# Moving early zero stores and weight loads between steps of one DMA queue: gated linear attention followed by a top-2 expert router on one core

## The chip, the core and the metric

The kernel runs on one core of one Trainium2 chip. The core has a matrix engine (TensorE, "PE" in the profile, with "PEld" for its weight loads), three engines for elementwise work (VectorE "DVE", ScalarE "ACT", GpSimd "POOL") and SyncE ("SP"), which here does nothing but send DMA transfers. POOL also sends DMA transfers, the indirect ones that gather or scatter rows by an index list. All transfers of the core run on the same 16 DMA engines. The metric is the device time of one execution in microseconds (us); lower is better.

## The reference, cut to what matters

There are two blocks. The first is a recurrent attention over 4 batches, 8 heads, 768 positions and a head width of 48:

```python
f = 1.0 / (1.0 + np.exp(-f_logit))
for t in range(S):
    state = f[:, :, t, :, None] * state + np.einsum('bhd,bhe->bhde', k[:, :, t], v[:, :, t])
    y[:, :, t] = np.einsum('bhd,bhde->bhe', q[:, :, t], state)
```

Its output is reshaped to x with 3072 tokens of 384 features. The second block is a router with 8 experts, each of which is a 384 x 1024 x 384 network with a ReLU. For every token the two experts with the largest noisy logits are chosen and weighted by a softmax over the two:

```python
noisy_logits = x @ w_gate + np.log1p(np.exp(x @ w_noise)) * noise
# top2, top2_w: the two largest and their softmax weights
for e in range(E):
    for k in range(2):
        mask = top2[:, k] == e
        out[mask] += top2_w[mask, k, None] * (np.maximum(x[mask] @ w1[e], 0.0) @ w2[e])
```

All data are float32.

## The kernel before, in words

**Attention.** The sequence is cut into 6 chunks of 128 positions; chunk and batch together give NS = 24 blocks, n = 4 * chunk + batch. The loop at line 1285 runs steps i = -3 to 25. In each step seven stages run, each on a block of its own: `forget(i+3)`, `scaled(i+1)`, `scores(i)`, `summed(i+2)`, `output(i-1)`, `decays(i+2)`, `features(i-2)` (a stage whose block does not exist is skipped). So `output(n)` is in step n+1 and `features(n)` in step n+2. `features(n)` (line 629) makes the 128 rows of x that belong to block n in the tile `xs`; they are stored to the DRAM buffer `x_rows` by SP, in the step that follows (the list `xw`, line 639).

**The order of the queue.** `in_order` (line 1205) keeps each engine's instructions in the order in which the program was written, so SP's transfers go out in exactly this order. In each step SP sends the loads of f, q, k and v for blocks three to four ahead (`load`, line 525, 192 KB each, in runs of 192 bytes), the store of the last step's x rows (line 639, 192 KB), in some steps a small load of noise (line 505), and then what the lines 1310 to 1318 add. Those lines are what the change touches. They send two kinds of transfers for which nothing in the attention waits:

- `zeros(count)` (line 1250) stores zeros into `count` blocks of 128 rows of the output (line 1254, 192 KB each). The results of the experts are later added into those rows, so the zeros have to be there first. The first twelve such stores cover the rows of the first half of each batch (chunks 0 to 2), the other twelve the second half. In the kernel before, the first twelve are sent in steps 6 to 13 (one each, after `output(5)` to `output(12)`) and in steps 22 and 23 (two each). The other twelve are sent after the loop, in the expert stage (line 1363).
- `part_of_weights(k, which, part)` (line 838) loads a quarter, 384 KB, of the first or second weight matrix of expert k. Expert 0's w1 goes in steps 14 to 17, one part each; its w2 in steps 18 and 19, two parts each (one after `output`, one after `features`); expert 1's w1 in steps 22 to 25.

**Routing.** After each chunk, `route(c)` (line 642) picks the two experts of each token and hands out eight indirect stores (`put`, line 708, sent by POOL at line 710), which write the tokens into the experts' lists in DRAM. When the lists of chunks 0 to 2 are written, the first expert pairs can begin although the attention still runs: `first_loads` (line 1259) sends, on SP, the look-up of the first 256 entries of expert 0's list (`fetch`, line 815, tile `slots`), then on POOL the gather of the token rows (`gather`, line 826, tile `xg`, in two halves of 128 tokens), and lets PE transpose the rows (`turned`, line 862, tile `xgp`). The look-up for expert 0 comes in step 20, right behind that step's store of x rows and its load of v. Its gather comes in step 21, its first transposes in step 22 after `output(21)`; steps 22 to 25 then hold both the last attention blocks and the first matmuls of expert 0 (line 914).

**Experts.** After the loop the list of items runs: four experts on their first 256 tokens, and then all experts on the rest, with products arranged in seven instead of eight multiplications (lines 939 and 1021). Each item ends with indirect stores on POOL that add the rows into the output (line 1030); those of the first four experts wait for the first twelve zero stores.

Of the kernel before, what the change touches and what calls it, by code (L numbers as in the profile page):

```python
# [331 lines left out]
def kernel(  # L332
# [192 lines left out]
    def load(nm, n):  # L525
        c, b = n // B, n % B
        if n < NCH * B:
            nc.sync.dma_start(out=pads[nm][n % RING[nm]][:, :, 0:D],
                              in_={"f": f_logit, "q": q, "k": k, "v": v}[nm][b, :, c * C:(c + 1) * C, :].rearrange("h t d -> t h d"))

    def clamp(n, engine=nc.gpsimd):
        if n < NCH * B:
            raw = pads["f"][n % RING["f"]][:, :, 0:D]
            engine.tensor_scalar(raw, raw, XMIN, None, ALU.max)
# [303 lines left out]
    def part_of_weights(k, which, part):  # L838
        if which == 1:
            few = slice(part * FF // 4, (part + 1) * FF // 4)  # L840
            nc.sync.dma_start(out=w1[k][:, :, few], in_=moe_w1[k].rearrange("(k p) f -> p k f", p=128)[:, :, few])
        else:
            few = slice(part * FO // 4, (part + 1) * FO // 4)
            nc.sync.dma_start(out=w2[k][:, few], in_=moe_w2[k].rearrange("(f p) d -> p f d", p=128)[:, few])
# [389 lines left out]
    NS = NCH * B  # L1234
# [15 lines left out]
    def zeros(count):  # L1250
        for _ in range(count):

            m = (*(m for m in range(NS) if m % NCH < HALF), *(m for m in range(NS) if m % NCH >= HALF))[len(zeroed)]
            zeroed.append(nc.sync.dma_start(out=out[m * 128:(m + 1) * 128, :], in_=zero))
            if m % NCH >= HALF:
                tc.declare_no_dep(zeroed[-1].ins, group="first half", reason="rows differ")
                tc.add_to_no_dep_group("second half", zeroed[-1].ins)
# [27 lines left out]
    for i in range(-3, NS + 2):  # L1285
        for stage, lag in ((forget, -3), (scaled, -1), (scores, 0), (summed, -2), (output, 1), (decays, -2), (features, 2)):
            n = i - lag
            if not 0 <= n < NS:
                continue
            stage(n)  # L1290
            if stage is forget:
                load("f", n + 4)
                clamp(n + 2, nc.gpsimd if n else nc.vector)
            elif stage is scaled:
                for nm in "qk":
                    load(nm, n + 2) if n < 4 else load(nm, n + 3)
                    if n == 3:
                        load(nm, n + 3)
                if n < 2:
                    load_router(n)  # L1300
                while xw:
                    xw.pop(0)()
            elif stage is scores:
                for m in (n + 1,) if n < 4 else (2 * n - 3, 2 * n - 2) if n < 6 else (n + 3,):
                    load("v", m)
                if n in (2, 6, 7, 8, 9, 10):
                    load_router(2 + (2, 6, 7, 8, 9, 10).index(n))
                elif n == 5:
                    nc.sync.dma_start(out=lists.rearrange("(p r) w -> p r w", p=128), in_=empty)
            elif stage is output:  # L1310
                if 5 <= n < 13:
                    zeros(1)
                elif n in (21, 22):
                    zeros(2)
            for when, first_n, last_n, whose, layer, part in ((output, 13, 16, 0, 1, 0), (output, 17, 18, 0, 2, 0),
                                                              (features, 16, 17, 0, 2, 2), (features, 20, 23, 1, 1, 0)):
                if stage is when and first_n <= n <= last_n:
                    part_of_weights(whose, layer, part + n - first_n)
            next(router, None)
            slot += 1  # L1320
            if puts and slot % (2 if n_routed == HALF else 3) == 0:
                puts.pop(0)()
            next(first_pairs, None)

            if done["turned"] and (n_first < 5 or i >= NS - 3 and stage is not forget) and (n_first < 11 or i >= NS - 1):
                next(pieces)
                n_first += 1
        if i < 0:
            warm_up(4)
        if i >= NS - 1:  # L1330
            while xw:
                xw.pop(0)()
        n = i - 2
        if n >= 0 and n % B == B - 1:
            c = n // B
            router = chain(router, route(c))
            n_routed = c + 1
            if c == HALF - 1:
                router = chain(router, enough())
                first_pairs = first_loads()  # L1340
            if c == NCH - 1:
                router = chain(router, plan(), beyond())
# [18 lines left out]
    for item, piece in pieces:  # L1361
# [6 lines left out]
        n = item - NE - 2  # L1368
# [52 lines left out]
```

## Time and profile before

| | |
|---|---|
| time, median of 3 runs | 662.32 us (660.88 to 662.96) |
| the profiled execution's own time | 667.17 us |
| its span, first to last instruction | 665.4 us |
| mean granted TensorE clock | 0.985 |
| ACT, POOL busy | 254.6 us (38%), 266.9 us (40%) |
| DMA, mean rate over the span | 145 GB/s |
| packets under 512 bytes | 115600 of 153897 |
| zero stores (`out_dram<-zero`) | 24, 192.0 KB each |
| weight parts (`w<-in_moe_w_dram`) | 16, 384.0 KB each |
| attention with DMA, 10 to 140 us | 132 to 230 GB/s in stretches of 10 us |

The durations come from one profiled execution, which took 4.85 us longer than the median of the timed runs. A line of a timeline gives the start in us from the span's start, the duration, the engine ("SPq" is SyncE sending a DMA), the line of the kernel, the operation, and the tiles as out<-in. For SPq the duration is the time for which SyncE was held by sending, not the time of the transfer. The chain of waits runs from the last instruction back to what released it. In the table by stretch, the last numbers are the granted clock of TensorE, the mean busy share of the DMA engines (the sum of packet times, so it can pass 1), and what they moved.

Step i is found in the trace by its scores (line 580): step 14's start at 92.76 us, step 19's at 125.09, step 20's at 130.69, step 22's at 141.04.

### The profile page before, as it was taken

The page shows a single profiled execution, that of the slowest core. Times are in us where ns is not written, and L with a number is a line of the kernel's source. Part 1 is how long each engine was busy: PE and PEld are TensorE (multiplying, and loading weights), DVE is VectorE, ACT ScalarE, POOL GpSimd, SP SyncE. Part 2 cuts the span into 40 slices and gives each one's busy share as a digit, 9 for nine tenths or more (in the row PEclk, how much of TensorE's full clock was granted, in tenths as well). Part 3 has the DMA queues.
Part 4 walks back from the last instruction along what each step waited for, and adds up shares of the span by engine and source line. Part 5 has one row for each costly group of instructions (what it writes and reads, how often), then busy time and mean ns, then how long its engine had stood idle before and what let it go on. Part 6 is the DMA issues. An engine that isn't in the chain of part 4 may idle for free.

```text
span 665.4 us, 12898 instructions
## 1 busy us (share of the span) xinstructions
PE 637.2 (96%) x4883; PEld 550.1 (83%) x4883; DVE 441.8 (66%) x993; ACT 254.6 (38%) x603; POOL 266.9 (40%) x300
## 2 busy tenths in 40 slices
PE   7999999967999999999999999999999999999991
PEld 7999988856999998999858965995698579889891
DVE  7777867853457666787666676757576667766751
ACT  5876766731221233333233333333322332232320
POOL 7633888715077623261521450325034214413021
PEclk9999999997999999999999999999999999999997
DMA  9999887893599423465725760836184337602112
GB/s 183 190 220 230 187 168 150 186 250 101 168 330 224 106 47 69 118 184 201 222 86 170 170 167 25 292 46 189 26 288 97 91 116 211 180 3 25 22 25 29
DMA packets 153897, 96.31 MB, mean 145 GB/s; under 512 B 115600, under 2 KB 146320, under 8 KB 153824
## 3 DMA queue, kind: packets, MB, share of 16 engines
q1 hardware_dynamic: 141648, 76.12, 41.6%
q0 software_dynamic: 12176, 19.25, 15.3%
q8 instruction: 41, 0.67, 0.4%
q14 instruction: 32, 0.26, 0.1%
HBM read 75.97 MB, written 19.62 MB: 144 GB/s over the span
## 4 chain that ended last, share of the span: by engine, by line
PE 93%; DMA 3%; issue 1%; DVE 1%; POOL 0%; SPq 0%; ACT 0%; POOLq 0%; DVEq 0%
PE y L1021 32%; PE P L939 8%; PE hp L914 6%; PE W L939 5%; PE Z L939 5%; PE V L939 5%; PE X L939 5%; PE xp L633 4%; PE sc L580 4%; PE y L598 4%; PE xgp L862 2%; PE y L609 2%; PE kp L540 2%; PE fp L540 1%; PE qp L540 1%; PE ds L604 1%
## 5 line engine op out<-in xcount | busy, mean ns | idle before, releaser
L1030 POOL DMA_INDIRECT out_dram<-ys,slots x48 | 81.8, 1705 | 154.1 <-ACT ys L1088 131.8
L1021 PE MATMUL y<-qk_all,f_all 128*128 128x192 f32 x576 | 105.2, 327 | 0.0
L1021 PEld LDWEIGHTS y<-qk_all,f_all 128*128 128x128 f32 x576 | 93.3, 190 | 0.3 <-DVE f_all L1003 0.3
L826 POOL DMA_INDIRECT xg<-x_rows,slots x48 | 53.5, 1114 | 50.5 <-DMA slots<-lists 34.1
L1021 PE MATMUL y<-w,hs_b 128*128 128x192 f32 x320 | 59.1, 328 | 0.0
L710 POOL DMA_INDIRECT lists<-entry,sloti x48 | 52.0, 1083 | 10.3 <-issue 9.9
L1021 PEld LDWEIGHTS y<-w,hs_b 128*128 128x128 f32 x320 | 52.9, 190 | 0.9
L1162 POOL DMA_INDIRECT out_dram<-ys_q,slots_q x5 | 8.6, 1718 | 104.0 <-DVE ys_q L1160 104.0
L914 PE MATMUL hp<-xt_a,w 128*128 128x256 f32 x192 | 43.7, 383 | 0.0
L975 ACT ACTIVATE hs_b<-hs_b 128x256 f32<-128x256 f32 (+1 forms) x32 | 15.1, 472 | 71.7 <-DVE hs_b L955 68.4
L914 PEld LDWEIGHTS hp<-xt_a,w 128*128 128x128 f32 x192 | 35.8, 190 | 4.9 <-issue 0.3
L939 PE MATMUL X<-xt_a,w 128*128 128x256 f32 (+1 forms) x128 | 39.7, 432 | 0.0
L939 PE MATMUL Z<-xt_b,v_all 128*128 128x256 f32 (+1 forms) x128 | 39.7, 432 | 0.0
L583 DVE TENSOR_TENSOR A<-sc,causal 128x1024 f32<-128x1024 f32 x24 | 29.3, 1222 | 13.4 <-PE sc L580 7.3
L1088 ACT ACTIVATE ys<-ys,slots 128x384 f32<-128x384 f32 x24 | 14.8, 617 | 59.7 <-DVE ys L1087 49.5
L1080 DVE TENSOR_TENSOR ys<-P,y 128x192 f32<-128x192 f32 x24 | 8.5, 354 | 42.2 <-PE y L1021 29.0
L955 DVE TENSOR_TENSOR hs_b<-hs_a,X 128x256 f32<-128x256 f32 (+1 forms) x32 | 15.6, 487 | 29.9 <-PE X L939 29.8
L1021 PE MATMUL y<-w,f_all 128*128 128x192 f32 x192 | 35.1, 326 | 0.0
L862 PE MATMUL xgp<-ident,xg 128*128 128x128 f32 x144 | 24.3, 279 | 9.9 <-DMA xg<-x_rows,slots 9.9
L939 PEld LDWEIGHTS X<-xt_a,w 128*128 128x128 f32 x128 | 24.3, 190 | 10.1
L939 PEld LDWEIGHTS Z<-xt_b,v_all 128*128 128x128 f32 x128 | 24.3, 190 | 10.1
L955 DVE TENSOR_TENSOR hs_a<-hs_a,P 128x256 f32<-128x256 f32 (+1 forms) x64 | 31.1, 486 | 1.4
(199 smaller groups left out, 1445.1 us busy)
## 6 DMA issues: line engine op xcount, KB each, us to landing
w<-in_moe_w_dram SPq DMA_DIRECT2D x16, 1536.0 KB
w_q<-in_moe_w_dram SPq DMA_DIRECT2D x10, 1536.0 KB
w<-in_moe_w_dram SPq DMA_DIRECT2D x16, 384.0 KB
f_all<-in_f_logit_dram SPq DMA_DIRECT2D x24, 192.0 KB
qk_all<-in_q_dram SPq DMA_DIRECT2D x24, 192.0 KB
qk_all<-in_k_dram SPq DMA_DIRECT2D x24, 192.0 KB
v_all<-in_v_dram SPq DMA_DIRECT2D x24, 192.0 KB
x_rows<-xs SPq DMA_DIRECT2D x24, 192.0 KB
```

Source lines behind the costliest of these rows:

```text
L540: nc.tensor.transpose(p[:, cols(hp)], flat[:, cols(hp)], ident)
L580: nc.tensor.matmul(sc[:, par, cols(hp)], lhsT=kQ[n][rows(par), cols(hp)], rhs=qP[n][rows(par), cols(hp)], start=True, stop=True)
L583: nc.vector.tensor_tensor(A[n].rearrange("j r (a i) -> j (r a) i", i=C), sc.rearrange("j r (a i) -> j (r a) i", i=C), causal.unsqueeze(1). ...
L598: nc.tensor.matmul(at(hp, par), lhsT=vt[:, 2 * hp + par, :], rhs=A[n][:, par, cols(hp)], start=(hp < 2), stop=(c == 0 and hp >= HP - 2))
L710: into = nc.gpsimd.indirect_dma_start(out=lists, out_offset=bass.IndirectOffsetOnAxis(ap=sloti[:, r, b:b + 1], axis=0), in_=entry[:, c, b, ...
L826: nc.gpsimd.indirect_dma_start(out=xg[p][:, s, :], out_offset=None, in_=x_rows[0:HALF * B * C] if p < NE else x_rows, in_offset=bass.Indir ...
L862: nc.tensor.transpose(xp[:, i * 128:(i + 1) * 128], xg[p][:, s, i * 128:(i + 1) * 128], ident)
L914: nc.tensor.matmul(hp[:, o, :], lhsT=w1[home(k)][:, i, (fo + o) * 128:(fo + o + 1) * 128], rhs=xt_a[:, i, k % 2 * 256:(k % 2 + 1) * 256], ...
L939: nc.tensor.matmul(to, lhsT=x, rhs=y, start=start, stop=stop)
L955: nc.vector.tensor_tensor(to, x, y, ALU.add)
L1021: nc.tensor.matmul(P[name], lhsT=x[:, o, :], rhs=y[:, o, :], start=(o == 0), stop=(o == FH - 1))
L1030: into = nc.gpsimd.indirect_dma_start(out=out, out_offset=bass.IndirectOffsetOnAxis(ap=slots[p][:, s, 2:3], axis=0), in_=ys[s], in_offset= ...
```

## The change

The twelve early zero stores leave steps 6 to 13, 22 and 23 and go, four each, into steps 22, 23 and 24 (after `output(21)` to `output(23)`). The four parts of expert 0's w1 move from steps 14 to 17 to steps 8, 10, 12 and 14. The four parts of its w2, sent two each in steps 18 and 19, are sent one each in steps 16, 17, 18 and 19. Expert 1's w1 stays in steps 22 to 25; it is only written differently. No computation changes, and no transfer is added or left out.

```diff
             elif stage is output:
-                if 5 <= n < 13:
-                    zeros(1)
-                elif n in (21, 22):
-                    zeros(2)
-            for when, first_n, last_n, whose, layer, part in ((output, 13, 16, 0, 1, 0), (output, 17, 18, 0, 2, 0),
-                                                              (features, 16, 17, 0, 2, 2), (features, 20, 23, 1, 1, 0)):
-                if stage is when and first_n <= n <= last_n:
-                    part_of_weights(whose, layer, part + n - first_n)
+                if n > NS - 4:
+                    zeros(NS // 6)
+                if n in (7, 9, 11, 13):
+                    part_of_weights(0, 1, (n - 7) // 2)
+                elif 15 <= n < 19:
+                    part_of_weights(0, 2, n - 15)
+            if stage is features and n >= NS - 4:
+                part_of_weights(1, 1, n - NS + 4)
             next(router, None)
             slot += 1
```

What each step's extra transfers are, in KB, before and after:

| step | 6, 7 | 8 | 9 | 10 | 11 | 12 | 13 | 14 | 15 | 16, 17 | 18, 19 | 22, 23 | 24 | 25 |
|---|---|---|---|---|---|---|---|---|---|---|---|---|---|---|
| before | 192 | 192 | 192 | 192 | 192 | 192 | 192 | 384 | 384 | 384 | 768 | 768 | 384 | 384 |
| after | 0 | 384 | 0 | 384 | 0 | 384 | 0 | 384 | 0 | 384 | 384 | 1152 | 1152 | 384 |

## The prediction

> **What bounds the kernel.** I read the busy rows first, then PE's waits, the chain, SyncE's timeline, and the table by stretch.
>
> ```profile
> PE 637.2 (96%) x4883; PEld 550.1 (83%) x4883; DVE 441.8 (66%) x993; ACT 254.6 (38%) x603; POOL 266.9 (40%) x300
> ...
> PE   7999999967999999999999999999999999999991
> ...
> PEclk9999999997999999999999999999999999999997
> ```
>
> PE is busy nearly everywhere; apart from the start, the only hole is in slices 9 and 10, some 140 to 160 us. PE's own waits say what that is:
>
> ```profile
> PE xgp L862 <- DMA xg<-x_rows,slots: 9.9, 1, 9.9
> PE fp L540 <- DVE f_all L534: 1.8, 2, 1.0
> ```
>
> One wait is worth 9.9 us; the next is at the start. So only a change to this wait can move the time by much. The chain shows what it consists of:
>
> ```profile
> 142.23 4.89 DMA slots<-lists
> 147.12 0.03 POOLq L826
> ...
> 147.93 4.85 DMA xg<-x_rows,slots
> 152.79 0.84 issue
> 153.63 0.87 PE xgp L862 x3
> ```
>
> PE has finished `output(21)` at 143.75 (the last y of line 609 starts at 143.08 and takes 0.67). SyncE sends the look-up of expert 0's list only at 142.23; it lands 4.89 us later, POOL starts the gather 0.81 after that, it lands in 4.85, and 0.84 later PE goes on: 11.40 us from look-up to PE. For no stall the look-up would have to go at 153.63 - 11.40 - 9.88 = 132.35. It belongs to step 20, whose scores start at 130.69, so it is sent some 10 us late. Why, SyncE's timeline shows:
>
> ```profile
> 92.51 1.12 SPq L1254 DMA_DIRECT2D out_dram<-zero  x1
> ...
> 98.95 3.94 SPq L841 DMA_DIRECT2D w<-in_moe_w_dram  x1
> ...
> 109.81 1.31 SPq L841 DMA_DIRECT2D w<-in_moe_w_dram  x1
> ...
> 138.43 2.73 SPq L844 DMA_DIRECT2D w<-in_moe_w_dram  x2
> 141.25 0.41 SPq L639 DMA_DIRECT2D x_rows<-xs  x1
> 141.76 0.38 SPq L528 DMA_DIRECT2D v_all<-in_v_dram  x1
> 142.23 0.88 SPq L815 DMA_DIRECT2D slots<-lists  x1
> ```
>
> SyncE is never idle here: one send follows the other, and sends that take 0.4 us when nothing holds them take 1 to 4. Compare each step's extra transfer with PE's first y (line 598) of that step, from the chain: step 13, 92.51 against 87.85, so SyncE is 4.7 us behind; step 14, 98.95 against 93.85: 5.1; step 15, 109.81 against 100.34: 9.5; step 16: 10.6; step 19, 138.43 against 126.19: 12.2; the look-up, 142.23 against 132.34: 9.9. The lag comes with the weight parts. What the look-up itself needs is ready far earlier: the last list store of chunk 2 is made by POOL at 127.95 and takes 1.68, and the store ahead of it needs ACT's xs of `features(17)`, done at 130.83 + 0.50 = 131.33. It waits for its turn in the queue, not for data.
>
> ```profile
> 130.00:140.00 10.00, 10.00 (x147) 8.80 (x146) 8.44 (x15) 5.79 (x17) 2.61 (x4) 1.00 0.88 207
> 140.00:150.00 10.00, 3.75 (x58) 3.05 (x56) 2.74 (x4) 2.92 (x9) 1.76 (x2) 0.89 0.91 268
> 150.00:160.00 10.00, 6.37 (x37) 5.79 (x38) 1.73 (x6) 0.48 (x1) 7.97 (x14) 0.60 0.54 137
> 160.00:170.00 10.00, 9.96 (x82) 8.15 (x83) 6.68 (x19) 2.83 (x6) 0.65 (x2) 1.00 0.12 40
> ```
>
> PE loses here 9.88 us of waiting plus a slower clock (0.60 granted). From 153.63 on, 3 + 3 transposes, 8 matmuls of xp and 16 of sc take 4.87 us (0.87 + 1.68 + 0.64 + 1.68); in earlier steps xp takes 1.07 and sc 1.09, and three transposes later take 0.33: 2.82 in all. So 2.0 us go to the clock: 11.9 us in all.
>
> **The change, part by part.**
>
> *Ahead of the look-up, fewer bytes.* Through step 19 the queue loses eight zero stores, 8 x 192 KB = 1.57 MB; all eight weight parts still precede the look-up. By steps: up to 13, three w1 parts (1.18 MB) replace eight zero stores (1.57 MB); step 14 keeps one part; steps 15, 18 and 19 lose one part each, 1.18 MB. From 98.95 to 142.23 SyncE sent 7.87 MB (8 weight parts, 6 row stores, and the f, q, k, v loads), 182 GB/s. At that rate 1.18 MB are 6.5 us, and the look-up would go at 135.7. Lower bound on the gain: only the SyncE time of three sends, 1.31 + 0.72 + 2.2 (the step 15 part, one of step 18 and the first of step 19) = 4.2. Upper bound: all 1.57 MB at that rate, 8.6, giving 133.6; that is still behind what the data allow (131.33 plus the store and the v load, some 132.3). I take 6.3: 135.9.
>
> *Its landing.* 4.89 us were measured with two w2 parts, a row store and a v load sent in the 3.8 us before. With one part less (0.39 MB, at the 268 GB/s of that stretch 1.5 us, of which not all was ahead) I take 1.2 less: 3.7. In an empty queue the look-up at 226.91 let its gather start at 229.42, so 2.5 is the shortest that the trace shows. Landing 139.6, POOL starts the gather at 140.4. POOL is free then: it idles from 136.89, and nothing on it is moved.
>
> *The gather.* Now four zero stores instead of two go out in steps 22 and 23, behind the row store of `features(19)`. That store needs an xs made at 141.64 to 142.12, so when SyncE is no longer late the zeros cannot go before 142.2; the first half of the gather, sent at 140.4, is under way. By the records of the trace the second half, sent at 150.57 as SyncE's queue ran dry, landed at 153.67, 3.1 us; the first half, with the queue full, took 4.85. I take 4.2: landed 144.6, PE at 145.4. The second half is sent 2.64 us later (147.93 to 150.57 now), at 143.0, into eight zeros and two weight parts (2.36 MB): 4.85 plus 0.84 gives 148.7, while PE, after three transposes and xp (1.4 us), wants it at 146.8. Stall 1.7 + 1.9 = 3.6 instead of 9.88: a gain of 6.3.
>
> The Trainium skill (DMA: Bandwidth & Descriptors, "Queues, rings and completion order") says each DMA engine alternates packet by packet between the queues that have work, so a deep SyncE queue would delay a gather little. The row says 4.85 against 3.1. By the rule alone the second half costs about 1.75 less; I keep the row.
>
> *The clock.* The skill (TensorE: Matmul & The Clock Gate, "Part 1: The HAM clock gate") says that after an idle window of about 3.4 us PE falls to half clock and needs as long to return. The row agrees for 9.88 us of idling (0.60 granted). With two stalls of under 2 us the rule gives back the whole 2.0; if one stall stays above 3.4 us, nothing, as the cost is the same for a short as for a long stall. I take 1.2 back. Total 7.5.
>
> *The zeros in steps 22 to 24.* Who waits: the first adding store (line 1030, at 189.05). The last four go behind the row stores of step 23, the second of which is sent at 167.66; four sends of some 0.46 end at 170, into stretches with a DMA share of 0.12 (160 to 170) and before the 1.5 MB load of expert 2's w1 (173.90). Slack 17 us, cost 0; if they did run into that load, 0.79 MB at the 358 GB/s of 180 to 190 is 2.2 us, ahead of expert 1's w1 (PE at 185.6). Expert 1's first two parts of w1 come later by four zero stores, 0.79 MB or 2.9 us at 268 GB/s, with 27 us to spare.
>
> *The w1 parts in steps 8, 10, 12.* Their tile is not in use, so they wait for nothing. Behind each in the queue are the loads of the next step, which PE needs three steps (18 us) later; a part of 384 KB every other step is the bytes of the zeros it replaces. Cost 0 while SyncE's lag plus the landing (5 us) stays below 18 us.
>
> **The sum.** Against the profiled execution (667.17 us, span 665.4): 667.17 - 7.5 = 659.7, span 657.9. It took 4.85 more than the median of 662.32; the stall is the same in both as far as I can tell, so 662.32 - 7.5 = **654.8 us**. After the stall PE has no DMA wait, so the gain should stay to the end.
>
> **Rivals.**
> (1) *The stall nearly vanishes*: the look-up goes at 133.6, lands in 3, both halves take about 3.1, and the clock stays up: up to 11.9, 650.4 to 652. For it: the data are ready at 132. Against it: the zeros meet the second half.
> (2) *The lag is made again*: SyncE's lag comes from the small-run loads and the list stores, which stay, and parts sent early hold it up as much as late ones. Then the look-up comes 0 to 4 us earlier: 658 to 662.3, that is no change at its end. For it: in steps 10 to 13 (zeros only) SyncE's steps already took 5.5 to 7.2 us against PE's 6.0 to 6.6.
> (3) *Slower*: each early w1 part holds SyncE like the first one in step 14, 3.94 us against a mean 0.83 for the eight zero stores. Less the zero of the step after, that is 2.3 more per pair of steps, 6.8 in three; minus the 4.2 saved, the look-up comes 2.6 later, and the lag after step 14 (5.1 + 6.8 + 4.4 = 16.3, plus 5 for landing) passes the 18 us of the q and k loads: 3 us of waiting on PE. 667 to 668. It decides once SyncE's lag at step 14 passes 5.1 + 6.3 = 11.4. Against it: the next three w1 parts took only 1.31 to 1.39 us.
>
> **Numbers.** The forecast's own case (gain 5 to 10, 652.3 to 657.3) has 0.52; (1) 0.14; (2) 0.22; (3) 0.12. A measurement of this kernel can tell about 0.3%, 2.0 us. Faster by more: 0.52 + 0.14 + 0.12 of (2) = 0.78; within: 0.10; slower: 0.12. The range leaves out (3) and the ends of (1) and (2): 650.0 to 662.3.
>
> **What would show it.** Right: the look-up sent at 134 to 138, on SyncE a lag under 6 us in step 19; PE's wait on xgp 1 to 5 us, perhaps in two pieces; a higher granted clock in 145 to 160; all after it earlier by the same amount. Wrong: SyncE's lag in step 14 above 10, PE waiting for q, k, v or f_all before 140; a gather that takes over 6 us; or a new PE wait behind line 914 or 1021 in which the gain is given back.

## The result, and the profile after

The change makes no difference that can be measured: 663.88 us median (658.26 to 667.28, 20 executions) against 663.70 (660.38 to 670.16, 20 executions) of the kernel before on the same chip, ratio 0.9991 (0.9971 to 1.0011). The forecast was 654.8. The profiled execution of the changed kernel took 664.42 us (span 662.7), 2.75 less than the profiled one of before. A ratio here and below is an estimate from the executions that lie within 1.5% of the fastest of their kernel, with its 95% interval, and not the quotient of the two medians, which are over all executions.

The measurements were made on six chips, called A to F here; A is that of the result. They differ by up to 1.3% for the same kernel, so times are compared on one chip only.

The page of the changed kernel on chip A, busy times and slices:

```profile
PE 640.4 (97%) x4883; PEld 553.8 (84%) x4883; DVE 445.5 (67%) x993; ACT 254.3 (38%) x603; POOL 266.8 (40%) x300
...
PE   8999999979999999999999999999999999999991
...
PEclk9999999997999999999999999999999999999996
```

PE's slices 9 and 10 show 7 and 9 where they showed 6 and 7; slice 10 of the clock row still shows 7. The hole has shrunk and is still there. PE's waits:

```profile
PE xgp L862 <- DMA xg<-x_rows,slots: 6.3, 2, 4.7
```

One wait of 9.9 us has become two, of 4.7 and 1.6 us. The chain shows the pieces:

```profile
137.74 4.49 DMA slots<-lists
...
143.04 1.02 POOL xg L826
...
145.67 6.36 DMA xg<-x_rows,slots
...
152.17 0.87 PE xgp L862 x3
153.04 2.01 PE sc L580 x16
155.05 3.94 PE hp L914 x12
```

The look-up goes 4.49 us earlier than before (142.23), lands in 4.49, and the first half of the gather, sent at 143.04, lands at 147.83. The second half, sent at 145.67, takes 6.36 us. PE starts the second half's transposes at 152.17, and then runs slowly: 16 of sc take 2.01 us and 12 of hp 3.94, where the third group of 12, from 164.27, takes 2.60. SyncE's timeline shows why the look-up is not earlier still:

```profile
99.94 2.75 SPq L841 DMA_DIRECT2D w<-in_moe_w_dram  x1
...
127.60 2.27 SPq L844 DMA_DIRECT2D w<-in_moe_w_dram  x1
...
131.89 3.19 SPq L639 DMA_DIRECT2D x_rows<-xs  x1
...
137.74 0.56 SPq L815 DMA_DIRECT2D slots<-lists  x1
```

A send of 0.34 us when nothing holds it still takes up to 3.19. I measure the lag from here on by one thing: the store of x rows (line 639) of each step against the start of that step's scores on PE, both by the timeline. In step 14 it is 5.1 us both before and after, in step 16 11.1 before and 9.0 after, in step 20 10.6 before and 6.4 after. The two stretches of 10 us with the stall:

```profile
140.00:150.00 10.00, 5.33 (x64) 4.66 (x63) 3.16 (x6) 2.85 (x9) 5.68 (x9) 0.86 0.84 259
150.00:160.00 10.00, 8.35 (x54) 6.47 (x54) 4.87 (x14) 1.07 (x2) 4.68 (x8) 0.63 0.54 130
```

The granted clock is 0.63 in 150 to 160, hardly more than the 0.60 of before. Finer stretches place it: it is 0.50 from 147.8 to 158.0 us before and from 147.1 to 157.3 after, 10.2 us in both.

A mark that serves in all that follows: the third group of 12 hp multiplications of expert 0 (line 914). By the timeline it starts at 166.69 us in the profile of before and at 164.11 in that of after, and from there to the end of the span it is 498.7 and 498.6 us. In these two profiles what happens behind it doesn't depend on the change; the time is decided by when PE comes to it.

### The profile page after: what moved, and what is told of

The parts are those of the page before. It is cut to its first block, busy times and chain, and to the rows that moved or that the text cites. A ratio compares the mean times of both kernels' runs of the same rounds, so it can differ in the third digit from the quotient of the medians.

```text
span 662.7 us, 12899 instructions
## 1 busy us (share of the span) xinstructions
PE 640.4 (97%) x4883; PEld 553.8 (84%) x4883; DVE 445.5 (67%) x993; ACT 254.3 (38%) x603; POOL 266.8 (40%) x300
## 4 chain that ended last, share of the span: by engine, by line
PE 92%; DMA 3%; DVE 1%; issue 1%; POOL 1%; ACT 1%; POOLq 0%; SPq 0%; DVEq 0%
PE y L1021 32%; PE P L939 8%; PE hp L914 7%; PE W L939 5%; PE Z L939 5%; PE V L939 5%; PE X L939 5%; PE sc L580 4%; PE xp L633 3%; PE y L598 3%; PE xgp L862 2%; PE y L609 2%; PE fp L540 2%; PE kp L540 1%; PE ds L604 1%; PE qp L540 1%
## 5 line engine op out<-in xcount | busy, mean ns | idle before, releaser
L710 POOL DMA_INDIRECT lists<-entry,sloti x48 | 53.6, 1117 | 11.8 <-issue 9.5
L1021 PEld LDWEIGHTS y<-w,f_all 128*128 128x128 f32 x192 | 31.9, 190 | 0.0
```

The lines of the kernel that those rows point to most:

```text
L710: into = nc.gpsimd.indirect_dma_start(out=lists, out_offset=bass.IndirectOffsetOnAxis(ap=sloti[:, r, b:b + 1], axis=0), in_=entry[:, c, b, ...
L1021: nc.tensor.matmul(P[name], lhsT=x[:, o, :], rhs=y[:, o, :], start=(o == 0), stop=(o == FH - 1))
```

## The experiments

### Which part of the change acts (chip B, kernel before 660.16 us)

Four kernels: the one before again, for a second trace, and the change in parts. The edit of the first part keeps the changed kernel's weights and puts all zero stores in one step:

```diff
-                if n > NS - 4:
-                    zeros(NS // 6)
+                if n == NS - 1:
+                    zeros(NS // 2)
```

The second has the zero stores of before with the weight parts of after, the third the weight parts of before with the zero stores of after.

> The kernel before, once more, for a second profile of the same instructions. If the profile of before was typical, the look-up is sent again at 141 to 143 us, PE's wait on xgp is again 9 to 10 us and the span about 665. If it was a draw from the slow end, the look-up comes earlier, the wait is 5 to 8 us and the span 661 to 663.

> The changed kernel with all twelve zero stores in step 24, none in steps 22 and 23. Theory A (the gain of the earlier look-up is eaten by gathers that run beside the zero stores): look-up unchanged at about 137.7, first half of the gather lands 3 to 4 us after its issue instead of 4.8, second half in 3 to 4 instead of 6.4, PE's two waits on xgp together 3 to 4 us instead of 6.3, time 2 to 4 us below the changed kernel (659 to 661). Rival B (the gather is slow for another reason, or the stall costs little in timed runs): waits stay at 6 us and the time within 1 us of the changed kernel.

> The kernel before with only the weight parts moved (steps 8, 10, 12, 14 and 16 to 19); the zero stores stay in steps 6 to 13, 22 and 23. Theory A: the queue is heavier in steps 8 to 14, so SyncE is later there; from step 15 on it catches up, the look-up goes at 138 to 141, the gather meets four zeros instead of eight, time 0 to 3 us below before. Rival C (the gain comes from fewer bytes ahead of the look-up, that is from the zeros alone): look-up at 141 to 143, time as before.

> The kernel before with only the zero stores moved to steps 22 to 24; the weight parts stay in steps 14 to 19. Theory A: SyncE starts step 14 less late, but has the same load after it, so the look-up goes at 139 to 142 and the gather meets eight zeros: time 0 to 3 us above the changed kernel. Rival C: look-up as early as in the changed kernel (137 to 139) and the time equal to it.

Measured: all zeros in step 24, 656.35, ratio 0.9944 (0.9913 to 0.9974); weights only 661.13, 1.0025 (0.9997 to 1.0054); zeros only 654.82, 0.9931 (0.9891 to 0.9971). The kernel before took 663.75 in its profiled execution; PE waits 9.3 us on xgp in it, nearly as long as on chip A. SyncE's timeline at the look-up, first in the kernel before:

```profile
140.21 0.88 SPq L815 DMA_DIRECT2D slots<-lists  x1
```

The same with weights only:

```profile
139.61 0.88 SPq L815 DMA_DIRECT2D slots<-lists  x1
```

And with zeros only, to which the four and four zero stores of steps 22 and 23 belong:

```profile
128.86 1.66 SPq L844 DMA_DIRECT2D w<-in_moe_w_dram  x2
...
133.92 0.37 SPq L815 DMA_DIRECT2D slots<-lists  x1
...
141.76 1.91 SPq L1254 DMA_DIRECT2D out_dram<-zero  x4
...
144.21 2.20 SPq L1254 DMA_DIRECT2D out_dram<-zero  x4
```

By these profiles, one of each kernel, spreading the weight parts is worth 0.6 us at the look-up, and it shows nothing in the time. Taking eight zero stores out of steps 6 to 13 is worth 6.3 us at the look-up, though two weight parts still go in step 19. The lag in step 14 shows where that comes from: it is 6.6 us in the kernel before, 8.0 with weights only and -0.3 with zeros only. From the first weight part of step 14 to the look-up it takes SyncE 39.5, 35.9 and 40.0 us: the spread weights do shorten that stretch by 3.6 us, but begin it 3.0 later, and the zeros that are gone let it begin 6.8 earlier. What the queue carries before step 14 thus reaches the look-up as a lag. At 133.9 to 134.0 (with all zeros in step 24, and with zeros only) it isn't held by SyncE any more: the last list store of chunk 2, made by POOL at 127.3 in the first and at 128.1 in the second, has landed at 133.9 in both.

None of the expectations came true as a whole: for the look-up that went at 133.9, theory A had 137.7 with the zeros in step 24 and 139 to 142 with zeros only, rival C 137 to 139.

So on this chip a part of the change gains what the whole did not gain on chip A; the whole was not run on chip B. In their profiled executions (658.3 with the zeros in step 24, 659.9 with zeros only) PE still waits 3.9 and 3.1 us on xgp, for the second half of the gather. With zeros only, this wait and the stretches of 5 us around it, in which the third number from the end is the granted clock:

```profile
PE xgp L862 <- DMA xg<-x_rows,slots: 3.1, 1, 3.1
...
145.00:150.00 5.00, 2.61 (x19) 2.29 (x19) 0.68 (x2) 0.08 (x1) 4.05 (x7) 0.63 1.01 306
150.00:155.00 5.00, 5.00 (x26) 3.82 (x24) 3.64 (x9) 0.49 (x1) 2.05 (x3) 0.69 0.74 205
```

The clock falls around this shorter wait too. The spread inside one kernel says more than its median: with the zeros in step 24, six executions took 653.4 to 654.6 and six 658.1 to 660.0; the kernel before has five of 24 under 657. The granted clock goes with it: 0.991 or more in the short ones, 0.990 or less in the long ones. I read them as executions in which PE does not idle long enough for its clock to fall, and executions in which it does; the profiles bear this out where there is one (in the four profiled executions with 0.992 or more, on chips E and F, PE never waits over 0.8 us on xgp). The table below counts them.

### The same on another chip (chip C, kernel before 668.38 us)

> The changed kernel again, on the same chip as the three that follow, since chips differ and the changed kernel has so far been compared only with before. Theory A (zeros beside the gather eat the gain): 2 to 4 us above the kernel with the zeros in step 24, and no faster than before. Theory D (early weight parts are the harm, whatever the zeros do): 3 to 5 us above the kernel with only the zeros moved. If both of those come out, the two are separate costs.

> Only the zero stores moved, weight parts in steps 14 to 19 as before; second time. Theory D: again 0.5 to 0.9% below before and below the changed kernel, with the look-up sent as soon as the list stores have landed (about 134). If the first result was luck of that chip's runs: within 0.2% of the changed kernel.

> The changed kernel with all twelve zero stores in step 24; second time. Theory A: again 2 to 4 us below the changed kernel, because the second half of the gather then lands 1 to 2 us earlier. If the look-up is again at 134 here and at 137 in the changed kernel, although both have the same queue up to it, the look-up's time varies between executions by some 4 us by itself.

The fourth had all twelve zero stores in step 24 with the weight parts of before:

> The kernel before with all twelve zero stores in step 24 and its own weight steps. Both harms taken away: if theories A and D both hold, the fastest of the four, 1 to 2 us below the kernel with only the zeros moved to steps 22 to 24 (652 to 655 on the chip of the first call). If the placement of the zeros in 22 to 24 costs nothing, equal to it.

Measured: the changed kernel 668.06, ratio 0.9968 (0.9943 to 0.9992); zeros only 0.9975 (0.9950 to 0.9999); zeros in step 24 0.9999 (0.9977 to 1.0020); with the old weights 0.9996 (0.9970 to 1.0021). The gain of chip B is all but gone (two of the ratios are 0.2 to 0.3% below 1), and neither theory A nor theory D shows: the four medians lie between 667.8 and 668.1. That is not because the look-up was late: in all four it goes at 133.8 to 136.0 and lands in 1.7 to 2.4 us, and no wait on xgp is left. PE's waits in the changed kernel on chip C show something else:

```profile
PE sc L580 <- issue: 3.0, 5, 1.0
```

PE's timeline there:

```profile
146.46 0.35 PE L580 MATMUL sc<-qP,kQ 64*128 64x128 f32 x1
147.18 0.39 PE L580 MATMUL sc<-qP,kQ 64*128 64x128 f32 x2 [0.38 <-issue]
148.60 0.80 PE L580 MATMUL sc<-qP,kQ 64*128 64x128 f32 x3 [1.03 <-issue]
150.01 1.09 PE L580 MATMUL sc<-qP,kQ 64*128 64x128 f32 x4 [0.62 <-issue]
151.46 0.80 PE L580 MATMUL sc<-qP,kQ 64*128 64x128 f32 x4 [0.35 <-issue]
152.88 0.78 PE L580 MATMUL sc<-qP,kQ 64*128 64x128 f32 x2 [0.62 <-issue]
```

Sixteen products of sc, which need 1.1 us elsewhere, take seven: two to four of them every 1.4 us, and in between PE waits for nothing that the trace shows ("issue"). I call this sparse issue. It lies at 142 to 155 us in the four profiles, the granted clock falls to 0.5 in it, and the third group of hp starts at 164.1 to 166.3 us, no earlier than with the gather's stall. Beside it POOL sends indirect transfers back to back, gathers and the eight list stores of chunk 3:

```profile
144.08 0.97 POOL L710 DMA_INDIRECT lists<-entry,sloti  x1 [0.22 <-issue]
...
145.35 0.97 POOL L710 DMA_INDIRECT lists<-entry,sloti  x1 [0.22 <-issue]
...
146.63 0.99 POOL L826 DMA_INDIRECT xg<-x_rows,slots  x1 [0.22 <-issue]
```

### Do the list stores cause the sparse issue? (chip D, kernel before 668.42 us)

The eight list stores of chunk 3 are held back until the loop is over:

```diff
-            if puts and slot % (2 if n_routed == HALF else 3) == 0:
+            if puts and len(n_put) < HALF * B * 2 and slot % (2 if n_routed == HALF else 3) == 0:
```

> The kernel before, for its trace on the chip of the other runs of this call. Theory A (between 140 and 155 us PE is held back either by the gather or, if the gather is early, by something that lets it issue only a few multiplications every 0.7 us; the two cover the same stretch): PE waits 9 to 10 us on xgp, and the third group of hp starts at 164 to 167 us. If this chip is like that of the call before (kernel before at 668), the look-up is sent at 134 to 141 us.

> Run again as a control for the next two: all twelve zero stores in step 24. It gave 0.9944 of the kernel before on one chip and 0.9999 on another. Theory A: between 0.994 and 1.000 again; where PE's issue is held back in 141 to 152 us it is near 1.000, where not it is near 0.994.

> The changed kernel with the eight list stores of chunk 3 sent after the loop instead of between the gathers of steps 21 to 25. Theory S (the dense run of indirect transfers on POOL, one every 1.28 us, is what holds PE's issue back and stretches the gather's second half): the stretch of sparse issue is gone, the second half of the gather lands in under 5 us, the third group of hp starts 4 to 6 us earlier than in the changed kernel, ratio to the kernel before 0.990 to 0.994. Theory F (the sparse issue has a cause outside of these stores): it stays at 142 to 155 us, ratio 0.997 to 1.000. If the stores only cost something wherever they are, the time comes back behind 165 us.

> The same edit on the kernel with all zero stores in step 24. Theory S: no sparse issue, xgp waits for 3 us or less, ratio 0.984 to 0.990. Theory F: as the control e1c, within 0.002 of it.

Measured: the control 667.38, ratio 1.0000 (0.9978 to 1.0022); the changed kernel without these stores 665.92, 0.9966 (0.9944 to 0.9987); zeros in step 24 without them 663.49, 0.9877 (0.9835 to 0.9919). That median is over six executions and the ratio from four of them (656.31, 657.48, 663.37 and 663.61, median 660.4); the other two took 670.13 and 670.93. The changed kernel with its stores was not run on this chip; on chip C its ratio is the same as that of the version without them here.

The kernel before is a surprise here. Theory A expected 9 to 10 us of waiting on xgp; it has none. Its look-up goes at 135.83 and lands 1.7 us later, SyncE's lag in step 20 is 0.7 us (chip A: 10.6), and what takes the place of the wait is sparse issue:

```profile
PE y L598 <- issue: 5.0, 7, 1.0
```

With the list stores gone from there, the sparse issue at 141 to 155 us is gone in both kernels; the third group of hp starts at 156.95 with the zeros in step 24, against 164.44 in the control. It is back where the stores went. In the changed kernel without stores in the loop, POOL sends 20 indirect transfers, 16 of them list stores, in the 28 us from 182.25 to 209.8, and PE, in the work of an expert:

```profile
205.61 0.93 PE L914 MATMUL hp<-xt_a,w 128*128 128x256 f32 x3
207.39 0.59 PE L914 MATMUL hp<-xt_a,w 128*128 128x256 f32 x2 [0.85 <-issue]
208.82 0.47 PE L914 MATMUL hp<-xt_a,w 128*128 128x256 f32 x1 [0.84 <-issue]
210.21 0.59 PE L914 MATMUL hp<-xt_a,w 128*128 128x256 f32 x1 [0.92 <-issue]
211.62 2.61 PE L914 MATMUL hp<-xt_a,w 128*128 128x256 f32 x4 [0.82 <-issue]
```

The same 1.4 us. So on this chip the sparse issue goes where the dense run of these stores goes, which speaks for theory S. Its numbers came true only in part: the ratio with the zeros in step 24 did (0.984 to 0.990 expected), that of the changed kernel did not (0.990 to 0.994). In the two profiles the price is paid again at 205 to 220 us (from the third group of hp to the end it is 505.7 and 511.5 us, 500.0 in the control), but both are of long executions: 670.20 us, the longest of twelve, and 670.13. Those of 656.31 and 657.48 can't have paid it: with 511.5 us behind it they would have come to that group at 143 and 144 us, an estimate, and the earliest in any profile is 153.07. So whether the price comes back varies by execution, and a profile without it there was not taken. That the stores stretch the second half of the gather, as theory S had it, is not confirmed: without them it took 5.99 us. In this profile of the changed kernel the look-up was late again (138.71, lag in step 20 6.9 us), although its SyncE queue is that of the changed kernel on chip C, with 1.3.

### The stores paced (chip E, kernel before 660.10 us)

Instead of moving the dense run, the eight stores are spread: none before step 23, and each waits on POOL for an x block of the steps 22 to 25.

```diff
-            n_put.append(c)
+            n_put.append(c), c == HALF and nc.gpsimd.tensor_copy(spacer, latest[0][0:1, 0, 0:1])
...
-        nc.scalar.copy(xs, xp[:, :, 0:XW])
+        nc.scalar.copy(xs, xp[:, :, 0:XW]); latest[:] = [xs]
...
-            if puts and slot % (2 if n_routed == HALF else 3) == 0:
+            if puts and (i >= NS - 1 or len(n_put) < HALF * B * 2 and slot % (2 if n_routed == HALF else 3) == 0):
```

> The changed kernel again, on the chip of the next three. Both theories: ratio 0.996 to 1.000.

> The kernel before with the eight list stores of chunk 3 held until step 23 and each made to wait on POOL for an x block of the steps 22 to 25, so that they go out one to three at a time over some 150 to 170 us. Theory S (the dense run of these stores holds back PE's issue): on a chip where the look-up is not late (landed by 138 us) the sparse issue goes, the third group of hp starts at 157 to 160 us instead of 164 to 166, ratio 0.988 to 0.992. On a chip where the gather is what ends the wait (PE waits over 8 us on xgp), little is gained: 0.996 to 1.000. If pacing only moves the price: 1.000.

> The changed kernel with the same pacing. If the sparse issue swallowed the forecast gain of 7.5 us: ratio to the kernel before 0.986 to 0.991, and better than the paced kernel before by up to 0.011 where that one still waits 8 us or more on xgp. If the gain never existed: 0.996 to 1.000, as the changed kernel.

> The kernel with all twelve zero stores in step 24 and the same pacing: no sparse issue and an undisturbed gather. Ratio 0.984 to 0.988, 0.002 to 0.004 below the paced changed kernel if the zero stores of steps 22 and 23 delay the gather's second half as in the profile of the changed kernel; equal to it if they don't.

Measured: the changed kernel, without any edit, 654.06 us, ratio 0.9933 (0.9897 to 0.9968). That is a gain of 6.0 us by the medians and 4.4 by the ratio (2.1 to 6.8), where the forecast had 7.5, and a miss for the expectation (0.996 to 1.000). The paced kernel before 657.45, 0.9964 (0.9924 to 1.0004); the paced changed kernel 653.37, 0.9923 (0.9888 to 0.9959); with the zeros in step 24 and paced 652.96, 0.9917 (0.9880 to 0.9955). Pacing and the place of the zeros are within the intervals of the plain change here; the 0.984 to 0.991 that theory S expected of them were not reached.

The two paced kernels differ by the change alone and have a profile each on one chip. PE's wait in the paced kernel before, and its chain at the look-up:

```profile
PE xgp L862 <- DMA xg<-x_rows,slots: 7.1, 1, 7.1
...
139.56 3.92 DMA slots<-lists
```

In the paced changed kernel:

```profile
PE xgp L862 <- DVE sp L658: 0.4, 1, 0.4
```

Its look-up goes at 133.89, 5.7 us earlier, with a lag in step 20 of 4.0 us instead of 8.5; the wait for the gather is gone, and the third group of hp starts at 153.07 instead of 161.63. So the chain that was forecast, from bytes to look-up to stall, does act on this chip. The medians, 657.45 and 653.37, differ by less than these two profiles, because the profile is of one of the long executions of before (661.38), and five of its twelve had, by their clock, no long wait either.

What chip E has and chip A had not, in the changed kernel: SyncE's lag in step 14 is much the same (4.5 us, 5.1 on chip A), but in step 20 it is 2.2 us instead of 6.4, the look-up goes at 133.37 instead of 137.74, the halves of the gather land in 3.1 and 4.1 us, and PE never waits over 0.8 us for xgp:

```profile
PE xgp L862 <- DVE nz L660: 0.8, 1, 0.8
```

What goes with the smaller lag shows in the stretches of 10 us, whose last number is GB/s. First the changed kernel on chip A:

```profile
80.00:90.00 10.00, 10.00 (x146) 9.14 (x145) 7.67 (x15) 7.00 (x18) 9.14 (x14) 1.00 0.76 149
90.00:100.00 10.00, 10.00 (x145) 9.06 (x142) 7.63 (x25) 7.81 (x23) 9.19 (x13) 1.00 0.85 164
100.00:110.00 10.00, 10.00 (x161) 9.07 (x158) 9.29 (x20) 6.26 (x17) 9.08 (x13) 1.00 0.76 149
110.00:120.00 10.00, 10.00 (x136) 9.18 (x136) 6.45 (x14) 7.93 (x23) 9.13 (x14) 1.00 0.84 175
120.00:130.00 10.00, 10.00 (x152) 9.07 (x148) 9.69 (x28) 7.38 (x20) 9.15 (x14) 1.00 0.86 191
```

The changed kernel on chip E:

```profile
80.00:90.00 10.00, 10.00 (x160) 8.90 (x158) 7.71 (x13) 6.45 (x16) 9.03 (x13) 1.00 0.88 187
90.00:100.00 10.00, 10.00 (x133) 9.18 (x132) 7.63 (x26) 8.59 (x24) 9.26 (x13) 1.00 0.77 158
100.00:110.00 10.00, 10.00 (x153) 9.19 (x152) 9.09 (x22) 6.42 (x18) 9.18 (x12) 1.00 0.85 174
110.00:120.00 10.00, 10.00 (x151) 9.19 (x149) 6.68 (x12) 7.69 (x22) 9.13 (x15) 1.00 0.91 194
120.00:130.00 10.00, 10.00 (x146) 9.06 (x142) 9.66 (x29) 6.70 (x18) 9.08 (x13) 1.00 0.91 209
```

The mean over these five is 166 GB/s on chip A and 184 on chip E, while PE runs at the same pace. Over 50 us, 18 GB/s are 0.9 MB, three quarters of the 1.18 MB that the change takes off the steps 15, 18 and 19. Chip E has no sparse issue either, although POOL sends its indirect transfers as densely as on chip C (ten in 137.72 to 150.84): PE is busy without a hole from 145 to 170 us.

### The look-up off SyncE's queue (chip F, kernel before 660.88 us)

```diff
-        got = nc.sync.dma_start(out=slots[p], in_=lists[row:row + 256, :].rearrange("(s p) w -> p s w", p=128))
+        got = (nc.gpsimd if p < NE else nc.sync).dma_start(out=slots[p], in_=lists[row:row + 256, :].rearrange("(s p) w -> p s w", p=128))
```

> The kernel before, with the look-ups of the first four experts' lists sent by POOL instead of SyncE; zero stores and weight parts as before. If the lag of SyncE's queue is what makes the look-up late: it goes when the last list store of chunk 2 has landed, 133 to 135 us, PE's wait on xgp falls to 0 to 3 us, and the ratio is 0.990 to 0.994 on a chip where the changed kernel gains, 0.996 to 1.000 where PE's issue is sparse between 141 and 155 us. If the traffic that SyncE's queue keeps on the DMA engines is the cause, and not the place in the queue: the look-up or the gather takes over 8 us to land, ratio 0.998 to 1.000.

> Look-ups by POOL, all twelve zero stores in step 24, weight parts as in the changed kernel, list stores of chunk 3 paced. Expected under the lag theory: no wait on xgp and no sparse issue, ratio 0.984 to 0.990 on any chip; no better than the paced version with zeros in step 24 (0.992) if the look-up there was early anyway.

Measured: the kernel before with this edit 663.86, ratio 1.0052 (1.0029 to 1.0074), slower; the version with all three edits 655.76, 0.9933 (0.9901 to 0.9965), a miss by its expected ratio. The first is no clean test. POOL's timeline shows that it put other work between look-up and gather:

```profile
135.00 0.82 POOL L815 DMA_DIRECT2D slots<-lists  x1 [4.35 <-DMA lists<-entry,sloti]
136.13 1.02 POOL L710 DMA_INDIRECT lists<-entry,sloti  x1 [0.30 <-DVE lg L636]
137.46 0.97 POOL L710 DMA_INDIRECT lists<-entry,sloti  x1 [0.30 <-issue]
138.45 1.70 POOL L625 TENSOR_TENSOR mid<-dss,st 128x256 f32<-128x256 f32 x1
...
141.15 1.01 POOL L826 DMA_INDIRECT xg<-x_rows,slots  x1 [0.31 <-DMA x_rows<-xs]
```

POOL waits 4.35 us for the list stores to land, sends the look-up at 135.00, and then has two list stores and a state update ahead of the gather, which goes at 141.15; its second half then takes 5.77 us and PE waits 1.9 and 3.3 us, 5.2 in all, where 0 to 3 were expected. The look-up itself takes 5.67 us to land on this queue, until 140.67, much the time at which POOL is through with that work, so the two can't be told apart. It shows that an early look-up alone doesn't bring an early gather, and leaves the lag theory where it was. In the version with all edits the look-up goes at 134.61 and lands in 3.56, the gather goes at 138.44 and 140.23, and PE waits 0.2 us for it.

### The executions behind the medians

Executions with a mean granted clock of 0.991 or more are, as read above, those in which PE has no long idle time; on chips B, E and F they are, with two exceptions in over a hundred, those under 657 us. The four versions of chips C and D that the table leaves out had none in twelve each.

| chip | kernel | median us | ratio (95%) | clock 0.991 or more |
|---|---|---|---|---|
| A | changed | 663.88 | 0.9991 (0.9971, 1.0011) | 0 of 20 |
| B | before | 660.16 | | 5 of 24 |
| B | weights only | 661.13 | 1.0025 (0.9997, 1.0054) | 0 of 12 |
| B | zeros only | 654.82 | 0.9931 (0.9891, 0.9971) | 5 of 7 |
| B | zeros in step 24 | 656.35 | 0.9944 (0.9913, 0.9974) | 6 of 12 |
| C | before | 668.38 | | 0 of 35 |
| C | changed | 668.06 | 0.9968 (0.9943, 0.9992) | 0 of 12 |
| D | before | 668.42 | | 0 of 23 |
| D | changed, stores after the loop | 665.92 | 0.9966 (0.9944, 0.9987) | 0 of 12 |
| D | zeros in step 24, stores after the loop | 663.49 | 0.9877 (0.9835, 0.9919) | 2 of 6 |
| E | before | 660.10 | | 7 of 34 |
| E | before, paced | 657.45 | 0.9964 (0.9924, 1.0004) | 5 of 12 |
| E | changed | 654.06 | 0.9933 (0.9897, 0.9968) | 9 of 12 |
| E | changed, paced | 653.37 | 0.9923 (0.9888, 0.9959) | 10 of 12 |
| E | zeros in step 24, paced | 652.96 | 0.9917 (0.9880, 0.9955) | 10 of 11 |
| F | before | 660.88 | | 5 of 23 |
| F | before, look-up on POOL | 663.86 | 1.0052 (1.0029, 1.0074) | 0 of 12 |
| F | zeros in 24, paced, look-up on POOL | 655.76 | 0.9933 (0.9901, 0.9965) | 12 of 12 |

The change doesn't shorten every execution by a little: where it helps, it makes the executions without a long wait more frequent, from 7 of 34 to 9 of 12 on chip E. The fastest executions there are alike, 653.06 before and 652.87 after. The version with the zeros in step 24 and paced stores is the fastest by median, but its interval overlaps that of the plain change, and it was not run on the chips with sparse issue.

## Why the prediction was wrong, point by point

The chain of the forecast held where PE waited on xgp: an earlier look-up, a shorter wait. Three steps of its sum failed on chip A: the bytes ahead of the look-up, with what follows from its time (a stall of 3.6 us was to be left, 6.3 were), the clock (1.2 us were to come back, 1.4 more were lost), and the step from the profiled execution to the median (the whole gain was carried over; 2.75 us between the two profiled executions became none between the medians).

- **What bounds the kernel**: right for the profile of chip A, where PE's one long wait is on xgp, and where what comes behind it takes the same time before and after. Not right for every chip: on D the kernel before has no such wait, and sparse issue holds PE in the same stretch. The profile of before could not show this.
- **Ahead of the look-up, fewer bytes**: the first of the steps that failed, by its size. It gave 6.3 us (135.9) between bounds of 4.2 and 8.6; chip A shows 4.49 (137.74), and against the start of step 20, which itself came 0.6 earlier, 3.9. Taken as the forecast took it, from the weight part of step 14 to the look-up, SyncE sent 6.68 MB in 37.8 us where it had sent 7.87 in 43.3: 5.5 us less, at 177 GB/s instead of the 182 that the step took as given. The other 1.0 is that this execution came to step 14, and already to step 6, 1.0 us later. The same kernel was served at 191 GB/s or more in that stretch on chip E, where the look-up went at 133.37. At 6.68 MB the difference between 177 and 191 is 2.8 us, nearly half of the saving. The split was wrong too: the saving was put on the weight parts of steps 15, 18 and 19, and what is ahead of step 14 at nothing, but on chip B the weights alone brought 0.6 us and the zeros alone 6.3, as a smaller lag in step 14. The data bound was off as well: some 132.3 assumed, 133.4 to 134.2 measured on chips B and E where SyncE was not late. The 1.68 us that were read for the last list store of chunk 2 are POOL's time for sending it; it takes some 6 us to land, in the profile of before until 133.9.
- **Its landing**: 3.7 forecast, 4.49 measured.
- **The gather**: 4.2 and 4.85 forecast, 4.79 and 6.36 measured, and the stall 6.3 instead of 3.6. The look-up's 1.8 us, the landing's 0.8 and the first half's 0.6 all fall into the first wait, 4.67 instead of 1.7; the second, 1.65, is what was forecast (1.9). That the zero stores beside it delay the second half is not what the runs say: on chip B it took 5.94 without any zeros there and 4.93 with eight, in the paced kernels of chip E 3.48 and 3.68. The 3.1 us that the forecast read for the second half in the profile of before were short: the trace keeps a completion 3.66 us after its issue. The gather's first half took 3.1 to 4.2 us in the five profiles of chips B and E in which SyncE's lag in step 21 was 1.3 or less, and 4.8 to 5.8 in those of A, B, D and E in which it was 2.5 or more. The rule of the Trainium skill (DMA: Bandwidth & Descriptors, "Queues, rings and completion order") that was weighed against the row fits the first kind; the row of before belongs to the second. A late look-up thus also meets a slow gather.
- **The clock** is the second step that failed: 1.2 us were to come back, and 1.4 more were lost. From the end of `output(21)` to the third group of hp, PE's work without the waits takes 14.5 us after and 13.1 before. The clock is at 0.50 for 10.2 us in both, but before 5.8 us of these passed in waiting, and after only 2.5; the rest fell on work. The skill's rule (TensorE: Matmul & The Clock Gate, "Part 1: The HAM clock gate") fits the first of the two stalls, 4.67 us, which is over its idle window. But its answer to stalls of under that window, nothing lost, which the forecast weighed in, is not what the runs show: with zeros only on chip B PE waited 3.09 us once and had a clock of 0.50 for the 6.8 us from 146.3, and with the look-up on POOL on chip F the clock was 0.50 from 146.4 on, after a wait of 1.92 us and as the second began. Nor was the cost the same for a short as for a long stall: with the zeros in step 24 on chip B, 0.50 lasted 3.4 us behind a wait of 3.92. Where no wait on xgp lasts over 0.8 us (the changed kernel on chip E) the clock is 1.00 throughout 140 to 170 us.
- **The sum**: between the profiles, the third group of hp came 2.6 us earlier instead of 7.5: 0.5 from before the stall, 3.6 from the waits (6.3 forecast), less 1.4 from the clock (1.2 forecast the other way). The third step that failed took these 7.5 us from the median, on the ground that the stall is the same in the profiled execution as in the others. It doesn't seem to have been. From the third group of hp to the end it is 498.7 us in both profiles of chip A, and an execution's time is 1.8 above its span; so the median execution of before should come to that group at 663.7 - 1.8 - 498.7 = 163.2, an estimate, 3.5 earlier than the profiled one (166.69), and that of after at 163.5, much the same place. What the median execution waited for was not seen. Part of it lay ahead of the stall: in the profile of before PE lost 0.6 us in 90 to 120, and step 20 began 1.7 later than in the second profile of before, on chip B, where step 6 began at the same time.
- **The zeros in steps 22 to 24, and the w1 parts in steps 8 to 12**: cost 0, as forecast. On chip A the rest of the execution is equally long, the lag in step 14 is 5.1 us in both, and after the change PE is busy 10.00 of 10 us in each stretch from 80 to 140.
- **The rivals**: in time chip A went by rival (2), the lag made again, at its end without a gain; it had 0.22, of which 0.12 were counted as faster and 0.10 as within 0.3%. In mechanism it went by it only in part: the look-up came 4.49 us earlier, more than its 0 to 4, and the lag in step 20 fell from 10.6 to 6.4. Rival (1), the stall nearly gone, is what chip E shows: 654.06, with nine of twelve executions at 652.9 to 655.3. Rival (3), slower by the early w1 parts, was seen nowhere: it needed a lag of 11.4 us in step 14, and the largest of any profile is 9.9.

What stays open: why the queue is served at different rates, and why some chips have the sparse issue with the same dense run of list stores and others not. The two may belong together: in the six profiles with sparse issue before 155 us SyncE's lag in step 20 is 0.6 to 1.3 us, the smallest of all. On chip A neither was tried with edits; that the late look-up keeps the gain away there rests on its one profile.

## What to carry to other kernels

A lag in a queue is a difference between what is asked of it and the rate at which it is served; before a gain is computed from the bytes taken off, compare the rate over several executions, since eight per cent of it over some 37 us came to nearly half of the saving here; and count the lag that the queue brings into the stretch, not only the bytes within it. Where a wait also costs clock, as the waits of 1.92 us and more did here and those of 0.8 and less did not, the times can fall on two levels and the median jumps between them: forecast how often the wait will be long, not its mean. And before one wait is taken as the bound of a stretch, ask what else would stand in that stretch if it were gone: here PE's own sparse issue beside a dense run of indirect stores gave the same end on two chips.

## What the runs showed of the hardware that was not expected

- On two of the six chips (C and D) PE issued only one to four multiplications per 1.4 us beside a dense run of indirect transfers on POOL, one every 1.28 us, while it waited for nothing that the trace shows. On chip D it went away with the eight list stores taken out of the run, and came back, in two long executions, where 16 stores ran together. On chip E the same run left PE at full pace.
- The last list store of chunk 2, 128 rows of 16 bytes, needed 5.7 to 7.5 us from its issue on POOL to its landing in the twenty profiles, which alone holds the look-up until 133 to 136 us.
- The same program was served 166 GB/s on one chip and 184 on another over the same 50 us; SyncE's lag in step 20 in the kernel before was 10.6, 10.3 and 0.7 us on chips A, B and D.
- The granted clock fell to 0.50 around waits of 1.92, 3.09 and 3.92 us too, and stayed there for 6.8, 6.8 and 3.4 us; around the stalls of 9.88 us and of 4.67 and 1.65 us on chip A it was 10.2.
